# One core, attention and a feed-forward layer: source order on all engines, and seven block products from chunk 12 on

## The chip, the core and the metric

The kernel runs on one core of a Trainium2 chip. The metric is the device time of one execution in microseconds. The core's engines each follow a queue of instructions of their own: PE multiplies matrices, DVE and ACT work on tiles of 128 partitions, POOL takes some elementwise work, SP issues the DMAs. They wait for each other by semaphores.

## The reference

```python
def _attn_ref(q, k, v, omega):            # q, k, v: (8, 8, 576, 64), omega: (128, 64)
    q_s, k_s = (q * scale, k * scale)
    def phi(x):
        proj = np.einsum('bhsd,md->bhsm', x, omega)
        sq = np.sum(x * x, axis=-1, keepdims=True) / 2.0
        h = proj - sq
        h = h - np.max(h, axis=-1, keepdims=True)
        return np.exp(h) / np.sqrt(m)
    q_p, k_p = (phi(q_s), phi(k_s))
    kv = np.einsum('bhsm,bhsd->bhmd', k_p, v)
    z = np.sum(k_p, axis=2)
    num = np.einsum('bhsm,bhmd->bhsd', q_p, kv)
    den = np.einsum('bhsm,bhm->bhs', q_p, z)[..., None] + 1e-06
    return num / den

def _moe_ref(x, w_in, w_out):             # x: (4608, 512), w_in: (512, 2048), w_out: (2048, 512)
    h = x @ w_in
    sp = np.where(h > 20.0, h, np.log1p(np.exp(np.minimum(h, 20.0))))
    g = h * np.tanh(sp)                   # mish
    return g @ w_out
```

The attention's output, heads side by side, is x of the feed-forward layer.

## The kernel before

The 4608 tokens are 36 tiles of 128 (t) and 18 chunks of 256 (c). Fp32 values are split into two fp16 halves, a rounded one (`cast`) and what it leaves (`rest`), and a product is three fp16 matmuls: low by high, high by low, high by high.

**Attention.** `q_task` runs once for each tile t, `k_task` for each batch b and pair of heads hp (32 of them). Both start in `features`: the input is split (ACT casts sq or sk, POOL makes the rest), PE multiplies with omega into two (q) or three (k) banks named pq and pk of the pool ps_a, DVE takes the maximum of each bank and subtracts it, ACT takes the exponential (eq, ek). A q task then has a cast (ACT) and rest (DVE) named qn, a transposing DMA into qp, PE's pn (with kv) in two banks of ps_a, and on DVE rd, its reciprocal and x, which frees the bank. x is split into xs and sent by a transposing DMA into xT. A k task has kp in the same way, vf scaled on ACT, its cast vb on DVE and rest on POOL, and PE's pkv.

**Feed-forward.** For each chunk `ff_in` makes h = x w_in into banks ph of the pool ps_h (two banks): eight groups of 24 matmuls 128x256. ACT's mish reads a bank one slot later, and `g_split` makes g's two halves a slot after that (cast on ACT, rest on DVE). `ff_out` multiplies the chunk ahead of it with w_out into po, 12 matmuls 128x512 a slot.

**Seven products.** From chunk SC0 on `ff_in7` takes its place. Both operands are cut into 2x2 blocks, and seven products of half size (Strassen's, in Winograd's form) do the work of eight: 24 matmuls 128x128 for each product, for each half of the features (gr 0 and 1), so 336 a chunk. It needs sums of w_in's blocks, s1 to s4, which `s_make` builds once in four parts (gr, hb): ten adds on DVE, four casts on ACT and four rests on DVE for each part, sent to HBM (ds) and loaded back from there for each use by `ask_sum` into a ring of three places in weight slots (rows w<-ds). It needs sums of x's blocks too (`x_sums`, tiles xm). Each product has a bank p_... of ps_a, and DVE adds the banks up in fp32 tiles h.

**Order.** The program is written in slots: `step` runs the pieces of tasks that are due, and each slot has a piece of `ff_in` (i) or of `ff_out` (o). From chunk 2 on the loop at the end of the kernel starts tasks when `pace` allows, and within what the data allow the scheduler of the language's tile layer chooses the order in which instructions stand on each engine. `s_make` starts at four slots, 11 apart, in chunks 11 to 13.

```python
    for i in range(4):
        at(slot[0] + 16 * (SC0 - 6) + 2 + 11 * i, lambda i=i: start(s_make(i // 2, i % 2)))
```

## Time and profile before

| | us |
|---|---|
| three runs | 962.81, 964.0, 983.06 (median 964.0) |
| profiled execution | 962.69 |
| its span | 960.8 |
| busy in the span: PE, DVE, ACT, POOL | 940.9, 624.9, 633.9, 222.7 |
| PE matmuls | 8568 |
| po, all matmuls | 375.2 |
| ph, all matmuls | 344.8 |

In the profile a group is written as line, engine, operation, output <- inputs, and its shape. "Busy" sums the instructions' own lengths, and the lengths of matmuls in a row overlap; the distance from start to start says what one costs. "PEclk" is the granted clock of PE. In a stretch's row the numbers behind the span are the busy times of PE, PEld, DVE, ACT and POOL, with their counts of instructions, then the clock, the DMA share and GB/s. An arrow in square brackets names what ended an instruction's wait.

### The profile page before, as it was taken

The page shows a single profiled execution, that of the slowest core. Times are in us where ns is not written, and L with a number is a line of the kernel's source. Part 1 is how long each engine was busy: PE and PEld are TensorE (multiplying, and loading weights), DVE is VectorE, ACT ScalarE, POOL GpSimd, SP SyncE. Part 2 cuts the span into 40 slices and gives each one's busy share as a digit, 9 for nine tenths or more (in the row PEclk, how much of TensorE's full clock was granted, in tenths as well). Part 3 has the DMA queues.
Part 4 walks back from the last instruction along what each step waited for, and adds up shares of the span by engine and source line. Part 5 has one row for each costly group of instructions (what it writes and reads, how often), then busy time and mean ns, then how long its engine had stood idle before and what let it go on. Part 6 is the DMA issues. An engine that isn't in the chain of part 4 may idle for free. (4 is left out here: it accounts for less than half of the span.)

```text
span 960.8 us, 20397 instructions
## 1 busy us (share of the span) xinstructions
PE 940.9 (98%) x8568; PEld 679.3 (71%) x8568; DVE 624.9 (65%) x1080; ACT 633.9 (66%) x818; POOL 222.7 (23%) x141
## 2 busy tenths in 40 slices
PE   9999988999999999999999999999989999999998
PEld 6788873677677777777777777777756777777663
DVE  5879797587766666656575655788889656643330
ACT  4758875686877877768667775778776866332231
POOL 0000052242432322322133333222231332200000
PEclk9979999999999999999999999999999999999999
DMA  9866314431741346313431253423552145634410
GB/s 287 271 208 208 109 48 94 102 58 61 140 92 37 107 77 119 69 59 75 101 68 53 69 118 66 93 89 68 136 124 73 37 100 115 172 117 131 133 57 33
DMA packets 147403, 100.25 MB, mean 104 GB/s; under 512 B 112112, under 2 KB 124528, under 8 KB 147312
## 3 DMA queue, kind: packets, MB, share of 16 engines
q1 hardware_dynamic: 147312, 98.95, 41.2%
q8 instruction: 67, 1.10, 0.5%
q14 instruction: 24, 0.20, 0.1%
HBM read 58.95 MB, written 13.63 MB: 76 GB/s over the span
## 5 line engine op out<-in xcount | busy, mean ns | idle before, releaser
L858 PE MATMUL po<-wo,g 128*128 128x512 f16 x1632 | 375.2, 380 | 0.0
L689 PE MATMUL ph<-xT,w 128*128 128x256 f16 (+1 forms) x2816 | 344.8, 279 | 0.7 <-ACT xT L72 0.7
L689 PEld LDWEIGHTS <-w 128*128 128x128 f16 x2688 | 261.0, 98 | 47.3 <-issue 0.7
L858 PEld LDWEIGHTS <-g 128*128 128x128 f16 x1632 | 155.1, 98 | 163.9 <-issue 2.2
L83 DVE SCALAR_TENSOR_TENSOR g<-h,us,g 128x1024 f16<-128x1024 f32 (+3 forms) x92 | 120.2, 1316 | 36.8 <-ACT g L72 36.2
L834 ACT ACTIVATE h<-ph,us 128x512 f32<-128x512 f32 (+3 forms) x152 | 83.3, 573 | 77.6 <-PE ph L689 76.8
L81 POOL TENSOR_TENSOR sq<-fq,sq 64x1024 f16<-64x1024 f32 x31 | 69.0, 2227 | 159.1 <-issue 65.2
L81 POOL TENSOR_TENSOR sk<-fk,sk 64x1152 f16<-64x1152 f32 x24 | 60.5, 2520 | 111.5 <-ACT sk L72 86.9
L81 POOL TENSOR_TENSOR xs<-x,xs 128x512 f16<-128x512 f32 (+1 forms) x35 | 44.2, 1264 | 151.9 <-issue 68.0
L72 ACT ACTIVATE g<-h,us 128x1024 f16<-128x1024 f32 (+3 forms) x80 | 72.6, 932 | 1.2
L834 ACT ACT_TABLE_LOAD x55 | 70.6, 1283 | 1.0
L364 ACT ACT_TABLE_LOAD x53 | 68.0, 1283 | 4.2 <-DVE ek L358 3.3
L349 DVE TENSOR_REDUCE mxq<-pq 128x4 f32<-128x512 f32 x72 | 46.8, 682 | 31.7 <-PE pq L340 31.6
L792 PEld LDWEIGHTS <-w 128*128 128x128 f16 x1008 | 58.4, 98 | 5.9
L81 DVE TENSOR_TENSOR qn<-eq,qn 128x1024 f16<-128x1024 f32 x31 | 38.9, 1254 | 36.2 <-ACT qn L72 36.2
L349 DVE TENSOR_REDUCE mxk<-pk 128x4 f32<-128x512 f32 (+1 forms) x96 | 50.1, 548 | 18.0 <-PE pk L340 18.0
L834 ACT ACTIVATE h<-h,us 128x1024 f32<-128x1024 f32 (+2 forms) x16 | 14.7, 933 | 61.9 <-DVE h L801 61.9
L72 ACT ACTIVATE o<-po,us 128x512 f32<-128x512 f32 (+1 forms) x38 | 25.8, 680 | 40.1 <-PE po L858 40.0
L81 DVE TENSOR_TENSOR kp<-ek,kp 128x1152 f16<-128x1152 f32 x24 | 36.4, 1515 | 24.0 <-ACT kp L72 24.0
L364 ACT ACTIVATE eq<-eq,lnt 128x1024 f32<-128x1024 f32 x31 | 35.6, 1148 | 21.2 <-DVE eq L358 21.0
L81 POOL TENSOR_TENSOR vb<-vf,vb 128x640 f16<-128x640 f32 x24 | 39.4, 1641 | 40.6 <-DVE vb L74 28.7
L801 DVE TENSOR_TENSOR h<-p_s,h 128x512 f32<-128x512 f32 x30 | 20.2, 689 | 43.2 <-PE p_s L792 43.2
(140 smaller groups left out, 1156.9 us busy)
## 6 DMA issues: line engine op xcount, KB each, us to landing
w<-ds SPq DMA_DIRECT2D x48, 256.0 KB, 3.4
vf<-in_vL_dram SPq DMA_DIRECT2D x32, 325.0 KB, 3.3
fq<-in_qT_dram SPq DMA_DIRECT2D x36, 256.0 KB, 3.6
out_dram<-o SPq DMA_DIRECT2D x36, 256.0 KB, 2.3
fk<-in_kT_dram SPq DMA_DIRECT2D x24, 256.0 KB, 3.6
raw<-in_w_out_dram SPq DMA_DIRECT2D x5, 1024.0 KB, 8.9
wo<-in_w_in_dram SPq DMA_DIRECT2D x4, 1024.0 KB, 13.2
raw<-in_w_in_dram SPq DMA_DIRECT2D x4, 1024.0 KB, 15.2
```

The source lines that it names most:

```text
L72: act.activation(out, in_, AF.Copy, scale=scale)
L81: eng.tensor_tensor(out=out, in0=in_, in1=hi, op=ALU.subtract)
L83: eng.scalar_tensor_tensor(out=out, in0=in_, scalar=scale, in1=hi, op0=ALU.mult, op1=ALU.subtract)
L349: sub = dve.tensor_reduce(out=mx[:, lo:hi], in_=pp[:, :m, :], axis=AX.X, op=ALU.max, negate=by_act)
L364: last = act.activation(e, e, AF.Exp, bias=lnt)
L689: nc.tensor.matmul(out=ph[:, i, :], lhsT=wi(a, k, f) if c else wi0(k, f), rhs=xT[c][:, y, k, :] if c else xT0()[:, k, :], start=n == 0, st ...
L792: nc.tensor.matmul(out=ph[:, i, :], lhsT=left(gr, op_l, i, a, k), rhs=x_region(c, r)[:, y, k0 + k, :], start=n == 0, stop=n == len(mm) - 1,)
L801: dve.tensor_tensor(out=out, in0=bank, in1=in0, op=ALU.add)
L834: act.activation(h[:, :, lo:hi], ph[:, :, lo:hi], AF.Mish, scale=us[:, 0:1])
L858: nc.tensor.matmul(out=po[i], lhsT=gT[c, gr][:, a, f % FG, i * P:(i + 1) * P], rhs=wo(y, f), start=f == 0 and (a, y) == parts[0], stop=f = ...
```

## The change

Four things are changed together.

1. SC0 goes from 15 to 12: chunks 12, 13 and 14 also use the seven products. `s_make` starts in chunks 8 to 10, its four parts 12 slots apart, with each rest and each store one slot later than its cast.
2. From chunk 2 on PE, SP, DVE, ACT and POOL keep the order of the source (`manual_schedule`). Every chunk has 16 slots that alternate i and o, and q and k tasks begin at slots that a table `base` fixes (q 27 and 23 slots ahead of their chunk, k at two places of the 16). For the later tasks the gaps ahead of pkv and pn are 4 and 3 slots.
3. The products of `ff_in7` accumulate in place. Bank pa (of ps_h) takes a11 b11, then s2 t2, s3 t3 and a22 t4 on top; ACT casts it in between and mish reads it at the end. Bank pd takes s1 t1, then s4 b22; bank pb (of ps_a) takes a12 b21. DVE has three adds for each half chunk where it had seven.
4. Buffers: xT has two tiles, each large enough for x's sums too; xs three; the h tiles four in place of five; v loads are cut into one piece for each pair of heads (`v_unit`).

```diff
-    SC0 = 15
+    SC0 = 12
...
+    def v_unit(b, hp):
+
+        if hp == 0:
+            vstate[b] = ({}, None, None)
+            vm[b] = sb.tile([P, HP], F32, tag="vmx", name=f"vmx{b}", bufs=2)
+        vstate[b][0][hp] = t = fetch_v(b, hp)
+        yield 4
+        dve.tensor_reduce(
+            out=vm[b][:, hp:hp + 1], in_=t[:, :, 0:D], axis=AX.XY, op=ALU.max, apply_absolute_value=True
+        )
+        if hp < HP - 1:
+            return
+        am = sb.tile([P, 1], F32, tag="vam", name=f"vam{b}")
+        dve.tensor_reduce(out=am, in_=vm[b], axis=AX.X, op=ALU.max)
+        allm = over_partitions(am, f"v{b}")
+        yield 1
+        p, s = pow2_of(allm, f"v{b}", TOP)
+        vstate[b] = (vstate[b][0], p, s)
+
...
-        yield gap("kv", f"k{b}_{hp}")
+        if b > 1 and b + 1 < B and hp + 1 < HP:
+            start(v_unit(b + 1, hp + 1), 2)
+        yield KV_GAP if nth >= LATE else gap("kv", f"k{b}_{hp}")
...
-        yield 2
+        yield QP_GAP if nth >= LATE else 2
...
+    REGION = ((0, 4), (1024, 4), (2048, 4), (3072, 2))
+
+    def x_tile(c):
+        if c not in xT:
+            xT[c] = sb.tile([P, 3584], F16, tag="xT", name=f"xT{c}", bufs=2)
+        return xT[c]
+
+    def x_plain(c):
+        return x_tile(c)[:, 0:2 * KT * CH].rearrange("p (a k s) -> p a k s", a=2, k=KT)
 
...
-    SUMS = ("s2", "s3", "s1", "s4")
+    SUMS = ("s2", "s1", "s3", "s4")
...
         def send(op, src):
-            o = sb.tile([P, 2, n], F16, tag="xs", name=f"{op}_{gr}_{hb}", bufs=2)
+            o = sb.tile([P, 2, n], F16, tag="xs", name=f"{op}_{gr}_{hb}", bufs=3)
             cast(act, o[:, 0], src)
+            yield 1
             rest(dve, o[:, 1], src, o[:, 0])
+            yield 1
             sums[gr, hb, op] = dram.tile([P, 2, n], F16, name=f"d{op}_{gr}_{hb}")
             nc.sync.dma_start(out=sums[gr, hb, op], in_=o)
 
         tt(s, block(sl2, 0, 0), block(sl2, 0, 1), ALU.add)
         tt(u, block(sl2, 1, 0), block(sl2, 1, 1), ALU.add)
         tt(s, s, u, ALU.add)
-        send("s1", s)
-        yield 2
+        yield from send("s1", s)
+        yield 1
         tt(s, s, block(sl1, 0, 0))
         tt(s, s, block(sl1, 1, 0))
-        send("s2", s)
-        yield 2
+        yield from send("s2", s)
+        yield 1
         tt(u, block(sl1, 0, 1), s)
         tt(u, u, block(sl1, 1, 1), ALU.add)
-        send("s4", u)
-        yield 2
+        yield from send("s4", u)
+        yield 1
         tt(s, block(sl1, 0, 0), block(sl2, 0, 0))
         tt(u, block(sl1, 1, 0), block(sl2, 1, 0))
         tt(s, s, u, ALU.add)
-        send("s3", s)
+        yield from send("s3", s)
         did("sums")
 
...
-        def products(gr, op_l, op_r):
+        def products(bank, gr, op_l, op_r, first):
             r, k0 = right[op_r]
             mm = [(a, y, k) for a, y in ((1, 0), (0, 1), (0, 0)) for k in range(2)]
-            ph = ps_a.tile([P, FQ, P], F32, tag="a", name=f"p_{op_l}_{c}_{gr}")
             for i in range(FQ):
                 for n, (a, y, k) in enumerate(mm):
                     nc.tensor.matmul(
-                        out=ph[:, i, :], lhsT=left(gr, op_l, i, a, k), rhs=x_region(c, r)[:, y, k0 + k, :],
-                        start=n == 0, stop=n == len(mm) - 1,
+                        out=bank[:, i, :], lhsT=left(gr, op_l, i, a, k), rhs=x_region(c, r)[:, y, k0 + k, :],
+                        start=first and i == 0 and n == 0, stop=n == len(mm) - 1, skip_group_check=True,
                     )
             if op_l in SUMS:
-                ask_sum()
-            return ph
-
-        def add(out, in0, bank):
-            dve.tensor_tensor(out=out, in0=bank, in1=in0, op=ALU.add)
+                later(1, ask_sum)
+
+        def bank(pool_, tag, name):
+            return pool_.tile([P, FQ, P], F32, tag=tag, name=name)
+
+        def add(out, bank):
+            dve.tensor_tensor(out=out, in0=bank, in1=out, op=ALU.add)
 
         for gr in range(FT // FG):
             gT[c, gr] = sb.tile([P, 2, FG, CH], F16, tag="g", name=f"g{c}_{gr}", bufs=GB)
...
             c11, c12, c21, c22 = (x[:, :, o:o + P] for x in h for o in (0, P))
 
 
-            p1 = products(gr, "a11", "b11")
-            cast(act, c21, p1)
+            pa = bank(ps_h, "h", f"pa{c}_{gr}")
+            products(pa, gr, "a11", "b11", True)
+            cast(act, c11, pa)
+            pb = bank(ps_a, "a", f"pb{c}_{gr}")
+            products(pb, gr, "a12", "b21", True)
+            later(1, add, c11, pb)
             yield
-            add(c11, c21, products(gr, "a12", "b21"))
+            products(pa, gr, "s2", "t2", False)
+            cast(act, c12, pa)
+            pd = bank(ps_h, "h", f"pd{c}_{gr}")
+            products(pd, gr, "s1", "t1", True)
             yield
-            add(c12, c21, products(gr, "s2", "t2"))
+            products(pa, gr, "s3", "t3", False)
+            cast(act, c22, pa)
+            later(1, add, c22, pd)
             yield
-            add(c21, c12, products(gr, "s3", "t3"))
+            products(pa, gr, "a22", "t4", False)
+            mish7(sp, h[1], pa)
+            products(pd, gr, "s4", "b22", False)
+            later(1, add, c12, pd)
+            later(1, mish, sp, h[0], h[0])
+            later(2, g_split, c, gr, 1, sp, h[1])
+            later(3, g_split, c, gr, 0, sp, h[0])
             yield
-            p5 = products(gr, "s1", "t1")
-            add(c22, c21, p5)
-            add(c12, c12, p5)
-            yield
-            add(c12, c12, products(gr, "s4", "b22"))
-            later(1, mish, sp, h[0], h[0])
-            later(2, g_split, c, gr, 0, sp, h[0])
-            yield
-            add(c21, c21, products(gr, "a22", "t4"))
-            later(1, mish, sp, h[1], h[1])
-            later(2, g_split, c, gr, 1, sp, h[1])
-            yield
+
+    def mish7(sp, h, pa):
+
+        for us, lo, hi in sp:
+            if lo < P:
+                e = min(hi, P)
+                act.activation(h[:, :, lo:e], pa[:, :, lo:e], AF.Mish, scale=us[:, 0:1])
+            if hi > P:
+                b = max(lo, P)
+                act.activation(h[:, :, b:hi], h[:, :, b:hi], AF.Mish, scale=us[:, 0:1])
 
...
-    GB, HB, QB = 4, 5, 1
+    GB, HB, QB = 4, 4, 1
...
+    LATE, KV_GAP, QP_GAP = 17, 4, 3
 
...
-    def pace(c):
-
-        return 15 + (c - 1) * 4.0 if c < 5 else 31.0 + (c - 5) * 3.8
+    def CS(c):
+
+        return 65 + 16 * (c - 2)
 
...
+    items = [("q", t) for t in range(NT)] + [("k", b, hp) for b in range(B) for hp in range(HP)]
+    items.sort(key=lambda it: it[1] if it[0] == "q" else it[1] * S // P - 0.5)
+    F = len(FIRST)
+    base = {}
+    for it in items[F:]:
+        if it[0] == "q":
+            base[it] = CS(it[1] // 2) - (23 if it[1] % 2 else 27)
+    late = CS(NCH)
+    for it in reversed(items[F:]):
+        if it[0] == "k":
+            late = min(late, base["q", it[1] * S // P]) - 1
+            while (late - CS(0)) % 16 not in (1, 13):
+                late -= 1
+            base[it] = late
+    items[F:] = sorted(items[F:], key=lambda it: base[it])
+    begin = list(FIRST) + [base[it] for it in items[F:]]
...
-        at(slot[0] + 16 * (SC0 - 6) + 2 + 11 * i, lambda i=i: start(s_make(i // 2, i % 2)))
+        at(slot[0] + 16 * (SC0 - 6) + 12 * i, lambda i=i: start(s_make(i // 2, i % 2)))
+    own = ExitStack()
+    own.enter_context(tc.manual_schedule(engines={mybir.EngineType.PE, mybir.EngineType.SP, mybir.EngineType.DVE, mybir.EngineType.Activation, mybir.EngineType.Pool}))
     for c in range(2, NCH):
         fi, fo = (ff_in if c < SC0 else ff_in7)(c), ff_out(c - 1)
-        order = "io" * 8 if c < SC0 else "iioiioioioi" * 2
+        order = "io" * 8
         for j, what in enumerate(order):
-            if j % 2 == 0 and given[0] < min(pace(c + j / len(order)), len(items)):
+            while F <= given[0] < len(items) and begin[given[0]] <= slot[0]:
                 give()
             next(fi if what == "i" else fo, None)
-            if (j + 1) * 16 // len(order) > j * 16 // len(order):
-                step()
+            step()
         for gen in (fi, fo):
             next(gen, None)
```

Three places where the rows stand otherwise. The first is ACT where a part of the sums is made (s1 to s4 the casts of sums, eq and ek exponentials, ph a bank of h's product). Before, in chunk 11:

```order
L834 ACTIVATE h11_1_1_7902<-ph11_1_1_0_7903,us5_7387 128x2x192
L434 ACTIVATE vf7_3_8185<-vf7_3_8185,s_v7_8408 128x10x64
L72 ACTIVATE sq29_8150<-fq29_8046 64x1024
L364 ACT_TABLE_LOAD
L364 ACTIVATE eq27_7928<-eq27_7928,lnt_72 128x1024
L72 ACTIVATE s1_0_1_8010<-s0_1_8006 128x512
L72 ACTIVATE kv6_7053<-pkv6_3_7966 128x2x65
L72 ACTIVATE qn27_8043<-eq27_7928 128x1024
L834 ACT_TABLE_LOAD
L834 ACTIVATE h11_1_1_7902<-ph11_1_1_2_8015,us4_6150 128x2x64
L834 ACTIVATE h11_1_1_7902<-ph11_1_1_2_8015,us5_7387 128x2x192
```

After, in chunk 9:

```order
L72 ACTIVATE sk5_3_6293<-fk5_3_6148 64x1152
L72 ACTIVATE g9_0_6087<-h9_0_0_6088,us4_6082 128x1024
L72 ACTIVATE s3_0_1_6312<-s0_1_5954 128x512
L387 ACT_TABLE_LOAD
L387 ACTIVATE ek5_2_6233<-ek5_2_6233,lnt_72 128x1152
L72 ACTIVATE kp5_2_6315<-ek5_2_6233 128x1152
L457 ACTIVATE vf5_2_4642<-vf5_2_4642,s_v5_5299 128x10x64
L875 ACT_TABLE_LOAD
L875 ACTIVATE h9_0_1_6257<-ph9_0_1_0_6258,us4_6082 128x512
L875 ACTIVATE h9_0_1_6257<-ph9_0_1_2_6323,us4_6082 128x512
```

Before, the cast of a sum stands behind the exponential; after, the cast of s3 stands ahead of the table load and the exponential ek, and kp's cast, vf and the mish of ph9_0_1_0 stand behind those.

The second is DVE at the corresponding places (s0_1 the sum in the making, x21 and x27 the quotients that free pn's bank). Before:

```order
L358 TENSOR_TENSOR eq28_8099<-pq28_4_8110,mxq28_8100 128x512
L724 TENSOR_TENSOR s0_1_8006<-w1_107,w3_109 128x512
L724 TENSOR_TENSOR s0_1_8006<-s0_1_8006 128x512
L506 TENSOR_SCALAR rd27_8188<-pn27_0_8189 128x4
L81 TENSOR_TENSOR qn28_8216<-eq28_8099,qn28_8216 128x1024
L510 RECIPROCAL rd27_8188<-rd27_8188 128x4
L506 TENSOR_SCALAR rd27_8188<-pn27_1_8202 128x4
L511 TENSOR_TENSOR x27_8187<-pn27_0_8189,rd27_8188 128x256
L510 RECIPROCAL rd27_8188<-rd27_8188 128x4
L511 TENSOR_TENSOR x27_8187<-pn27_1_8202,rd27_8188 128x256
```

After:

```order
L381 TENSOR_TENSOR ek5_2_6233<-pk5_2_5_6247,mxk5_2_6234 128x512
L83 SCALAR_TENSOR_TENSOR g9_0_6087<-h9_0_0_6088,us4_6082,g9_0_6087 128x1024
L749 TENSOR_TENSOR s0_1_5954<-w1_76,w3_78 128x512 x2
L749 TENSOR_TENSOR s0_1_5954<-s0_1_5954 128x512
L74 CAST vb0_114<-vf5_2_4642 128x10x64
L81 TENSOR_TENSOR s3_0_1_6312<-s0_1_5954,s3_0_1_6312 128x512
L81 TENSOR_TENSOR kp5_2_6315<-ek5_2_6233,kp5_2_6315 128x1152
L529 TENSOR_SCALAR rd21_6349<-pn21_0_6350 128x4
L533 RECIPROCAL rd21_6349<-rd21_6349 128x4
L534 TENSOR_TENSOR x21_6348<-pn21_0_6350,rd21_6349 128x256
```

Before, two adds and qn's rest stand between the subtraction and x27; after, g's rest, three adds, vb's cast, the sum's rest and kp's rest stand between the subtraction and x21.

The third is DVE where the seven products' banks are added up (h15 and h12 the tiles of h). Before, in chunk 15, the first chunk with them:

```order
L511 TENSOR_TENSOR x34_10133<-pn34_0_10135,rd34_10134 128x256
L510 RECIPROCAL rd34_10134<-rd34_10134 128x4
L511 TENSOR_TENSOR x34_10133<-pn34_1_10148,rd34_10134 128x256
L74 CAST xs17_0_10190<-x34_10133 128x512
L801 TENSOR_TENSOR h15_0_0_10077<-p_s2_15_0_10195,h15_0_1_10078 128x4x128
L801 TENSOR_TENSOR h15_0_1_10078<-p_s3_15_0_10223,h15_0_0_10077 128x4x128
L801 TENSOR_TENSOR h15_0_1_10078<-p_s1_15_0_10266,h15_0_1_10078 128x4x128
L801 TENSOR_TENSOR h15_0_0_10077<-p_s1_15_0_10266,h15_0_0_10077 128x4x128
```

After, in chunk 12:

```order
L372 TENSOR_REDUCE mxk7_0_8331<-pk7_0_4_8341 128x1
L381 TENSOR_TENSOR ek7_0_8330<-pk7_0_4_8341,mxk7_0_8331 128x128
L372 TENSOR_REDUCE mxk7_0_8331<-pk7_0_5_8344 128x4
L381 TENSOR_TENSOR ek7_0_8330<-pk7_0_5_8344,mxk7_0_8331 128x512
L74 CAST vb0_114<-vf7_0_7021 128x10x64
L829 TENSOR_TENSOR h12_0_1_8141<-pd12_0_8253,h12_0_1_8141 128x4x128
L81 TENSOR_TENSOR kp7_0_8405<-ek7_0_8330,kp7_0_8405 128x1152
L529 TENSOR_SCALAR rd27_8466<-pn27_0_8467 128x4
```

Before, four adds of banks of ps_a follow x34 with nothing of another kind between them; after, the one add of pd12_0 stands behind vb's cast and ahead of kp's rest.

## The prediction

> **What bounds the kernel now.** I read the page's busy shares first, then the busy time by stretch (one stretch per chunk of 256 tokens), then PE's waits, and last the single instructions around the waits.

> ```profile
> span 960.8 us, 20397 instructions
> ...
> PE 940.9 (98%) x8568; PEld 679.3 (71%) x8568; DVE 624.9 (65%) x1080; ACT 633.9 (66%) x818; POOL 222.7 (23%) x141
> ```

> PE is the bound: 98% busy. So a change can win in two ways only: less matmul time, or PE's few idle stretches. The stretches below are chunk 6 (an ordinary one), 11, 12, 13 and 16; after the span come busy times of PE, PEld, DVE, ACT, POOL.

> ```profile
> 371.95:420.94 48.99, 48.99 (x468) 35.49 (x467) 29.80 (x62) 36.47 (x47) 13.40 (x9) 1.00 0.39 69
> 615.04:664.46 49.42, 49.42 (x480) 35.91 (x478) 42.59 (x71) 38.44 (x55) 15.16 (x10) 1.00 0.26 69
> 664.46:717.32 52.86, 50.38 (x452) 35.19 (x451) 49.52 (x81) 39.26 (x46) 14.95 (x8) 0.97 0.55 126
> 717.32:768.40 51.08, 49.58 (x479) 35.84 (x478) 38.23 (x55) 38.78 (x54) 11.97 (x7) 1.00 0.21 63
> 857.12:896.60 39.48, 39.48 (x436) 28.14 (x434) 14.04 (x20) 10.98 (x14) 0.00 (x0) 1.00 0.38 121
> ```

> Chunks 11 to 13 are where before builds the sums of weight blocks (s_make). DVE is there at 38 to 50 us a chunk where it has 30 ordinarily, and two of the three chunks are longer than chunk 6 by 2 to 4 us. That is the nearest thing the trace has to what the change will do in chunks 8 to 10. PE's waits from chunk 2 to the end, with totals, times and the longest:

> ```profile
> PE pk L340 <- DVE x L511: 2.7, 2, 2.4
> PE pkv L445 <- DVE kp L81: 1.9, 2, 1.5
> PE pn L495 <- DMA qp<-qn: 0.9, 1, 0.9
> ```

> They add up to 5.5 us. The longest, and what came around it, in PE's timeline (start, length, group; starts of successive groups give the true pace):

> ```profile
> 697.56 0.92 PE L495 MATMUL pn<-kv,qp 128*128 128x65 f16 x24
> 698.32 2.75 PE L858 MATMUL po<-wo,g 128*128 128x512 f16 x12
> 700.91 2.78 PE L689 MATMUL ph<-xT,w 128*128 128x256 f16 x24
> 703.53 0.72 PE L340 MATMUL pk<-om,sk 128*128 128x128 f16 x10
> 706.63 0.63 PE L340 MATMUL pk<-om,sk 128*128 128x128 f16 x8 [2.38 <-DVE x L511]
> 707.08 4.44 PE L858 MATMUL po<-wo,g 128*128 128x512 f16 x12
> ...
> 862.38 1.50 PE L792 MATMUL p_s<-xm,w 128*128 128x128 f16 x24
> 863.73 1.50 PE L792 MATMUL p_s<-xT,w 128*128 128x128 f16 x24
> ```

> Start to start: pn 0.76 us, po 2.59, ph 2.62, 24 matmuls of 128x128 1.35 (56 ns each), 8 of them 0.45. Behind the 2.38 us wait, po took 4.44 instead of 2.75: 1.69 us lost to a lower granted clock (0.97 over that chunk). So PE loses 5.5 + 1.7 = 7.2 us from chunk 2 on.

> Why PE waited there is the key to the forecast. The third bank of pk is one that pn held, and DVE's x frees it:

> ```profile
> 701.41 2.21 DVE L81 TENSOR_TENSOR s<-s,s 128x512 f16<-128x512 f32 x1
> ...
> 704.75 0.15 DVE L506 TENSOR_SCALAR rd<-pn 128x4 f32<-128x4 f32 x1
> 704.82 1.21 DVE L81 TENSOR_TENSOR qn<-eq,qn 128x1024 f16<-128x1024 f32 x1
> ...
> 706.14 0.42 DVE L511 TENSOR_TENSOR x<-pn,rd 128x256 f32<-128x256 f32 x1
> 706.49 0.17 DVE L510 RECIPROCAL rd<-rd 128x4 f32<-128x4 f32 x1
> ...
> 707.15 0.43 DVE L74 CAST xs<-x 128x512 f16<-128x512 f32 x1
> 707.49 1.28 DVE L83 SCALAR_TENSOR_TENSOR g<-h,us,g 128x1024 f16<-128x1024 f32 x1
> ```

> A sum's rest of 2.21 us, two adds and qn's rest stand ahead of x on DVE. Work of s_make ahead of x stops PE.

> **The change, part by part.** *Seven products in chunks 12 to 14.* Each of them had 8 groups ph of 24 matmuls 128x256: 8 x 2.62 = 20.96 us. It gets 2 x 7 x 24 = 336 of 128x128: 14 x 1.35 = 18.90. That is 2.06 less a chunk, **-6.2 us** in three. This lies on the path, since PE is the bound. [...]

> *Adds in place.* Accumulating in the bank replaces 7 DVE adds per half chunk by 3. DVE is at 14 of 39 us in chunk 16, so this is worth nothing there; what it puts in chunks 12 and 13 is priced below. The loads of the sums double to 96:

> ```profile
> w<-ds SPq DMA_DIRECT2D x48, 256.0 KB, 3.4
> ```

> Each is asked for one slot after a product, three products ahead of its use, some 11 us: with 3.4 us to land it is hidden. Behind SP's waits for a transpose (queue work that now stands in source order) that cover shrinks to 1.5 to 3 us; I price it at nothing, with a few us above.

> *Source order on all engines.* Before's order from chunk 2 on is made anew, so its three waits and the slow-clock stretch have no reason to be at the same places: **-7.2 us** at most, taken whole, since any new wait is priced by itself. In ordinary chunks (3 to 7, 11) I walked two chunks of the new order with the rows here: the banks of ph and pk come free at least 2.4 us ahead of PE. I cost that at nothing; the cover is this slack.

> *s_make in chunks 8 to 10.* DVE has about 30 us a chunk and gets nearly all of what chunks 11 to 13 had extra: 42.59 + 49.52 + 38.23 - 3 x 29.80 = 40.9 us in 48 slots of 3.06. By load alone (30 + 14 of 49) it fits. By order it doesn't. The last of a sum's four parts, in slots 181 to 184: ACT's cast of s3 stands ahead of the table load and exp of ek, and DVE's adds that it waits for stand behind g's rest. DVE's vb cast then waits for ACT's vf, and holds s3's rest, kp's rest and x21. The rows, by shape, of the stretch of chunks 11 to 13 (us busy, then mean ns):

> ```profile
> L349 DVE TENSOR_REDUCE mxk<-pk 128x4 f32<-128x512 f32 x14 | 9.5, 680 | 0.0
> L358 DVE TENSOR_TENSOR ek<-pk,mxk 128x512 f32<-128x512 f32 x14 | 9.5, 679 | 0.0
> L81 DVE TENSOR_TENSOR kp<-ek,kp 128x1152 f16<-128x1152 f32 x7 | 9.5, 1356 | 7.3 <-ACT kp L72 7.3
> L724 DVE TENSOR_TENSOR s<-w,w 128x512 f32<-128x512 f16 x8 | 5.5, 683 | 0.1
> L74 DVE CAST vb<-vf 128x640 f16<-128x640 f32 x6 | 2.9, 486 | 0.0
> L349 DVE TENSOR_REDUCE mxk<-pk 128x1 f32<-128x128 f32 x7 | 1.9, 278 | 0.0
> L358 DVE TENSOR_TENSOR ek<-pk,mxk 128x128 f32<-128x128 f32 x7 | 1.9, 277 | 0.0
> ...
> L364 ACT ACT_TABLE_LOAD x12 | 15.4, 1283 | 0.2
> L72 ACT ACTIVATE s<-s 128x512 f16<-128x512 f32 x16 | 10.0, 626 | 19.2 <-DVE s L724 10.8 <-POOL vb L81 3.8 <-DMA xT<-xs 2.9
> L364 ACT ACTIVATE ek<-ek,lnt 128x1152 f32<-128x1152 f32 x7 | 8.8, 1256 | 7.9 <-DVE ek L358 7.9
> L72 ACT ACTIVATE kp<-ek 128x1152 f16<-128x1152 f32 x7 | 8.1, 1152 | 0.0
> L434 ACT ACTIVATE vf<-vf,s_v 128x640 f32<-128x640 f32 x4 | 3.2, 830 | 0.0
> ```

> T = 0 is the end of x20's first half, which lets PE go on in slot 180. DVE: second half of x 0.74 (0.15 + 0.17 + 0.42), xs cast 0.43, a sum's rest 0.68 (as an undisturbed add of that size), three pieces of reduce and subtract 3.27, g's rest 1.28, three adds 2.05: 8.5. ACT: cast 0.63, table 1.28, exp 1.26, kp 1.15, vf 0.83: 13.6. DVE: vb 0.49, rest 0.68, kp's rest 1.36, rd, reciprocal and x 0.74: 16.9. PE meanwhile: 0.45, ph 2.62, po 2.59, ph 2.62, pn 0.76, po 2.59, ten of pk 0.56: 12.2. PE waits **4.7 us**. I walked slots 161 to 184 in this way, which hold two of the four sums; PE waits 0.5 (slot 164), 2.3 (168), 3.6 (173), 1.6 (177), 1.4 (180) and 4.7 (184): 14.1. The four come every 12 slots and the k and q tasks every 4, so the other two repeat it: **+28 us**. The bound below is nothing, if what I call ordered so tightly runs ahead of PE; above, rests and adds beside POOL at up to 2.2 us (the row at 701.41) instead of 0.68 raise the same walk to about 44 us. I take 28, the walk with undisturbed durations, because the only waits of this kind in the trace, 2.38 and the other 0.3 of pk's 2.7, came with a better order.

> *Chunks 12 and 13.* DVE's add of the s1 product (out of bank pd) stands behind the vb cast, and PE's s4 product goes into pd. Walked likewise from x: DVE 0.74 + 0.43 + 3.27 = 4.4, exp, kp and vf 3.2, vb and the add 1.2: 8.8. PE: 0.45 + 1.35 + 2.59 + 1.35 = 5.7. A wait of 3.0 in the first half of each: **+6 us** (0 if DVE is early, 10 with POOL beside it).

> *Clock.* Each wait of 2.4 us or more may cost 1.7 as at 707.08; six places walked are that long (two each of 3.6, 4.7 and 3.0): 0 to +10. [...] I put no term in, and let it carry the upper end.

> Sum: 960.8 - 6.2 - 7.2 + 28.1 + 6.0 = 981.5 of span; the profiled execution took 962.69, 1.9 more than its span: 983.4. The median of the runs shown is 964.0, 1.3 above the profiled one, so the figure is **983**, +2.0%.

> **The rivals.** *The engines keep up.* Only the products and the old waits count: 960.8 - 13.4 + 1.9 = 949, with a few short waits up to 966. For it: DVE 0.9 loaded at most, ACT 0.8, and before's chunk 11 lost only 0.4 us with 42.59 us on DVE. Against it: two engines that wait for each other within one slot, in an order nobody may leave, and the 2.38 us wait with less ahead of x.

> *Contended rests and the lower clock.* The place is the same, slots 161 to 208. If DVE's rests and g's rests run beside POOL's long ones, the walk gives 44 instead of 28, and the waits are long enough for the slower clock, 10 more: 960.8 - 13.4 + 44 + 6 + 10 + 1.9 = 1009. It decides from the point where a sum's rest takes over 1.5 us in most slots; in chunks 11 to 13 some did (2.21), some did not.

> *The in-place bank.* In chunks 12 to 17 PE's next product into pa waits for ACT's cast of it, twelve half chunks with some 2 us of slack. If ACT is late by 2 more each time, 24 us come on top of 949: 973. Against it: ACT at 11 of 39 us in chunk 16.

> *The weight load shows.* A load of weights is longer than the matmul it feeds:

> ```profile
> L689 PEld LDWEIGHTS <-w 128*128 128x128 f16 x2688 | 261.0, 98 | 47.3 <-issue 0.7
> ```

> If its 98 ns were not hidden, chunks 12 to 14 would have 336 x 98 = 32.9 us of products, 14.0 more each than priced: 983 + 42 = 1025. In chunk 16 it is hidden. [...]

> **How the numbers follow.** The walk (966 to 1000) has 0.58, the engines that keep up (946 to 966) 0.28, contended rests (over 1000) 0.08, the bank 0.05, the weight load 0.01. The likeliest gives 983, its own range 966 to 1000. The whole range takes in the upper part of the rival that is faster: **950 to 1000**. Two per cent, about what a measurement of this kernel can tell from no change, are 944.7 and 983.3. Below 944.7 the walk has nothing and the first rival only its edge: 0.03. Above 983.3 lies half of the walk (0.29), all of the contended case and the weight load (0.09) and some of the bank case: 0.42. Within: 0.55.

> **What would show it.** Right: PE waits in chunks 8 to 10 for DVE's x (pk) and ACT's mish (ph), 20 to 40 us in all, at the same places every 12 slots; ACT idle for s ahead of exp; chunks 12 to 14 near 47, 47 and 44 us. A wait at the s4 product in chunks 12 and 13. Wrong: chunks 8 to 10 at 49 us each, which would be the first rival; or chunks 3 to 7 over 49.5, for I gave them slack. If ordinary chunks wait, my walk of them was too kind, and if sums cost under 10 us, too harsh.

## The result and the profile after

The changed kernel takes 1025.78 us (median, 1023.89 the lowest) against 964.2 us of the kernel before: a ratio of 1.0637, 95% interval 1.0612 to 1.0662. The forecast was 983, the range 950 to 1000. In some executions the startup, up to chunk 0's first matmul of ph, takes some 17 us longer (64 us instead of 46.5); so times "from chunk 2 on" below go from chunk 2's first matmul of ph to the end of the span. They are 787.8 us before and 851.3 after. Each is of one profiled execution; the two profiles of one and the same kernel, e1 and e9 below, have 781.7 and 781.3.

The page after, busy times; PE has 432 more matmuls and is busy for 93% of the span instead of 98%:

```profile
span 1023.9 us, 21326 instructions
...
PE 956.5 (93%) x9000; PEld 692.9 (68%) x9000; DVE 622.2 (61%) x1092; ACT 639.1 (62%) x836; POOL 235.8 (23%) x147
```

DVE's and ACT's busy times are nearly as before (624.9 and 633.9), and POOL's, 13 us longer, is 23% of the span. So no engine has become too full: PE waits. Its waits from chunk 2 on (total, times, longest), which summed to 5.5 us before:

```profile
PE pk L363 <- DVE x L534: 14.7, 6, 4.7
PE pq L363 <- POOL sq L81: 13.5, 6, 5.4
PE pq L363 <- DVE ek L381: 9.2, 1, 9.2
PE ph L714 <- ACT h L875: 7.9, 4, 3.4
PE pd L818 <- DVE h L829: 5.6, 3, 2.8
PE pd L818 <- DMA w<-ds: 3.1, 3, 2.1
```

That is 54 us. The stretches show where: chunks 2, 3, 6, 8, 9, 10, 12 and 13 (after the span PE, PEld, DVE, ACT, POOL, then the clock):

```profile
172.56:237.15 64.59, 52.48 (x503) 38.25 (x501) 41.60 (x70) 40.06 (x47) 19.90 (x10) 0.95 0.31 72
237.15:289.43 52.28, 52.08 (x502) 37.50 (x501) 35.19 (x64) 41.58 (x47) 17.67 (x9) 0.96 0.32 81
387.34:436.22 48.88, 48.88 (x468) 35.39 (x466) 28.81 (x54) 37.90 (x51) 15.77 (x9) 1.00 0.37 88
488.22:546.83 58.61, 51.98 (x467) 36.76 (x466) 43.21 (x67) 36.10 (x40) 14.38 (x8) 0.95 0.32 87
546.83:611.05 64.22, 54.12 (x464) 38.27 (x464) 45.69 (x79) 42.77 (x49) 17.51 (x10) 0.88 0.38 93
611.05:670.24 59.19, 52.09 (x491) 36.85 (x490) 43.12 (x67) 35.54 (x39) 14.00 (x8) 0.95 0.34 81
724.12:774.60 50.48, 47.73 (x611) 36.15 (x610) 35.50 (x60) 32.27 (x38) 15.96 (x10) 0.99 0.66 148
774.60:827.32 52.72, 48.60 (x612) 36.67 (x610) 37.01 (x66) 35.48 (x43) 15.97 (x10) 0.97 0.63 149
```

Chunk 6, where no sums are made, runs at 48.88, as well as before. Chunks 8 to 10 take 182.0 us, 35.4 over three of that. In their rows PE's busy time is 3 to 5 us over chunk 6's, and the clock below 1: behind eleven of the waits PE's pace halves for a while. Summed over the starts of all matmuls these stretches cost 19.6 us (2.6 and 2.4 behind the waits of 9.2 and 4.7, 1.5 to 1.7 behind nine others; before, one of 1.7). Which waits have such a stretch behind them is in the last section.

The three largest kinds of wait, in the timelines of the changed kernel. First the one in slot 184 that the prediction walked, on PE, ACT and DVE:

```profile
571.83 0.72 PE L363 MATMUL pk<-om,sk 128*128 128x128 f16 x10
577.20 1.03 PE L363 MATMUL pk<-om,sk 128*128 128x128 f16 x8 [4.65 <-DVE x L534]
```

```profile
567.69 0.63 ACT L72 ACTIVATE s<-s 128x512 f16<-128x512 f32 x1 [5.72 <-DVE s L749]
568.34 1.28 ACT L387 ACT_TABLE_LOAD   x1
569.63 1.25 ACT L387 ACTIVATE ek<-ek,lnt 128x1152 f32<-128x1152 f32 x1
570.92 1.16 ACT L72 ACTIVATE kp<-ek 128x1152 f16<-128x1152 f32 x1
571.99 0.81 ACT L457 ACTIVATE vf<-vf,s_v 128x640 f32<-128x640 f32 x1
```

```profile
566.97 0.69 DVE L749 TENSOR_TENSOR s<-s 128x512 f32<-128x512 f32 x1
572.84 0.50 DVE L74 CAST vb<-vf 128x640 f16<-128x640 f32 x1 [5.18 <-ACT vf L457]
573.25 0.68 DVE L81 TENSOR_TENSOR s<-s,s 128x512 f16<-128x512 f32 x1
573.85 2.56 DVE L81 TENSOR_TENSOR kp<-ek,kp 128x1152 f16<-128x1152 f32 x1
...
576.72 0.42 DVE L534 TENSOR_TENSOR x<-pn,rd 128x256 f32<-128x256 f32 x1
```

DVE's add ends, ACT casts the sum, loads the table, takes exp, kp and vf; all that time DVE stands at vb's cast, with x behind it. Second, the wait of 9.2 us in chunk 2, on PE, ACT, DVE and SP (SP's row merges two transposes; a row of SP's length includes what the instruction waited):

```profile
235.49 1.87 PE L363 MATMUL pq<-om,sq 128*128 128x128 f16 x16 [9.24 <-DVE ek L381]
237.15 4.64 PE L714 MATMUL ph<-xT,w 128*128 128x256 f16 x24
```

```profile
229.99 1.06 ACT L72 ACTIVATE sq<-fq 64x1024 f16<-64x1024 f32 x1 [9.16 <-DMA fq<-in_qT_dram]
```

```profile
228.66 0.82 DVE L299 TENSOR_REDUCE vmx<-vf 128x1 f32<-128x640 f32 x1 [8.11 <-DMA vf<-in_vL_dram]
...
234.66 0.69 DVE L381 TENSOR_TENSOR ek<-pk,mxk 128x512 f32<-128x512 f32 x1
```

```profile
197.36 27.61 SPq L600 DMA_TRANSPOSE xT<-xs  x2
225.06 0.52 SPq L271 DMA_DIRECT2D vf<-in_vL_dram  x1
225.69 0.51 SPq L320 DMA_DIRECT2D fq<-in_qT_dram  x1
```

Two loads came late, vf and fq, issued at 225.06 and 225.69 behind a transpose that SP's waits list holds for 25.0 us against PE's ph. DVE stood 8.11 us at v's maximum for vf, and ek, which stands behind it, ended at 235.35; that is the last thing before PE went on at 235.49, as the profile says. ACT stood 9.16 us for fq; sq's rest on POOL ended at 233.82 (with DVE free, in e7, PE waits here for it alone, 7.2 us). The transpose writes tile 8's x into xT4, which now has the buffer of xT2, and chunk 2 still reads that. The ph row shows the lower clock: 4.64 instead of 2.78. Third, POOL ahead of a wait of pq for sq:

```profile
598.84 0.72 POOL L120 PARTITION_ALL_REDUCE allm_v<-vam  x1 [6.45 <-DVE vam L305]
607.19 2.12 POOL L81 TENSOR_TENSOR sq<-fq,sq 64x1024 f16<-64x1024 f32 x1 [7.63 <-issue]
```

Between v's maximum over partitions and the next instruction the profile has POOL idle for 7.6 us with nothing to wait for, and PE waits 5.4 us for sq. The gap was there before too, also ahead of a rest of sq, but no wait of PE came of it:

```profile
301.77 0.38 POOL L114 PARTITION_ALL_REDUCE allm_v<-vam  x1 [6.21 <-DVE g L83]
309.21 2.13 POOL L81 TENSOR_TENSOR sq<-fq,sq 64x1024 f16<-64x1024 f32 x1 [7.07 <-issue]
```

### The profile page after: what moved, and what is told of

Its sections match the earlier page's. It is cut to its first block, busy times and chain, and to the rows that moved or that the text cites. A ratio compares the mean times of both kernels' runs of the same rounds, so it can differ in the third digit from the quotient of the medians.

```text
span 1023.9 us, 21326 instructions
## 1 busy us (share of the span) xinstructions
PE 956.5 (93%) x9000; PEld 692.9 (68%) x9000; DVE 622.2 (61%) x1092; ACT 639.1 (62%) x836; POOL 235.8 (23%) x147
## 3 DMA queue, kind: packets, MB, share of 16 engines
q8 instruction: 70, 1.15, 0.5%
## 5 line engine op out<-in xcount | busy, mean ns | idle before, releaser
L714 PE MATMUL ph<-xT,w 128*128 128x256 f16 (+1 forms) x2240 | 291.7, 289 | 8.6 <-ACT h L875 7.9
L714 PEld LDWEIGHTS <-w 128*128 128x128 f16 x2112 | 211.6, 101 | 47.3 <-issue 9.1
L818 PEld LDWEIGHTS <-w 128*128 128x128 f16 x2016 | 117.5, 98 | 18.1 <-issue 5.9
L83 DVE SCALAR_TENSOR_TENSOR g<-h,us,g 128x1024 f16<-128x1024 f32 (+3 forms) x92 | 98.3, 1088 | 45.7 <-ACT g L72 45.0
L81 POOL TENSOR_TENSOR xs<-x,xs 128x512 f16<-128x512 f32 (+1 forms) x38 | 47.2, 1241 | 254.5 <-DVE xs L74 112.0
L81 POOL TENSOR_TENSOR sq<-fq,sq 64x1024 f16<-64x1024 f32 x31 | 67.9, 2191 | 93.2 <-ACT sq L72 43.9
L875 ACT ACTIVATE h<-ph,us 128x512 f32<-128x512 f32 (+3 forms) x120 | 64.2, 571 | 29.3 <-PE ph L714 28.7
L81 POOL TENSOR_TENSOR sk<-fk,sk 64x1152 f16<-64x1152 f32 x24 | 56.9, 2371 | 100.9 <-ACT sk L72 77.7
L81 POOL TENSOR_TENSOR vb<-vf,vb 128x640 f16<-128x640 f32 x24 | 48.7, 2028 | 106.8 <-DVE vb L74 97.1
L818 PE MATMUL pa<-xT,w 128*128 128x128 f16 x1152 | 72.9, 220 | 0.0
L72 ACT ACTIVATE g<-h,us 128x1024 f16<-128x1024 f32 (+3 forms) x80 | 71.6, 925 | 0.1
L81 DVE TENSOR_TENSOR qn<-eq,qn 128x1024 f16<-128x1024 f32 x31 | 37.9, 1222 | 51.4 <-ACT qn L72 51.4
L72 ACT ACTIVATE h<-pa 128x512 f32<-128x512 f32 x36 | 21.3, 590 | 73.4 <-PE pa L818 73.1
L387 ACT ACT_TABLE_LOAD x50 | 64.2, 1283 | 0.9
L363 PE MATMUL pq<-om,sq 128*128 128x128 f16 x496 | 36.6, 233 | 25.6 <-POOL sq L81 16.4
L363 PEld LDWEIGHTS <-sq 128*128 128x128 f16 x496 | 32.9, 105 | 34.6 <-POOL sq L81 19.6
L875 ACT ACT_TABLE_LOAD x43 | 55.2, 1283 | 0.8
L72 ACT ACTIVATE o<-po,us 128x512 f32<-128x512 f32 (+1 forms) x38 | 25.8, 678 | 45.1 <-DVE us L690 21.7
## 6 DMA issues: line engine op xcount, KB each, us to landing
w<-ds SPq DMA_DIRECT2D x96, 256.0 KB, 3.5
fq<-in_qT_dram SPq DMA_DIRECT2D x36, 256.0 KB, 4.0
out_dram<-o SPq DMA_DIRECT2D x36, 256.0 KB, 2.0
fk<-in_kT_dram SPq DMA_DIRECT2D x24, 256.0 KB, 3.7
raw<-in_w_in_dram SPq DMA_DIRECT2D x4, 1024.0 KB, 15.4
```

Source lines behind the costliest of these rows:

```text
L72: act.activation(out, in_, AF.Copy, scale=scale)
L81: eng.tensor_tensor(out=out, in0=in_, in1=hi, op=ALU.subtract)
L83: eng.scalar_tensor_tensor(out=out, in0=in_, scalar=scale, in1=hi, op0=ALU.mult, op1=ALU.subtract)
L363: nc.tensor.matmul(out=pp[rows, i, :], lhsT=left[:, o:o + rows.stop - rows.start], rhs=right, start=j == 0, stop=j == len(terms) - 1,)
L387: last = act.activation(e, e, AF.Exp, bias=lnt)
L714: nc.tensor.matmul(out=ph[:, i, :], lhsT=wi(a, k, f) if c else wi0(k, f), rhs=x_plain(c)[:, y, k, :] if c else xT0()[:, k, :], start=n == ...
```

## The experiments

Theory A: the fixed order makes PE wait, in three separate ways (A1 POOL's gap ahead of sq, A2 the transpose that blocks SP's loads, A3 the casts of sums ahead of exp on ACT) and one more (A4 vb's cast ahead of the add). Rival B: what costs is the rest of the change, the two xT tiles, the doubled loads of sums, or the banks that PE and ACT use in turn.

**e1: the whole change but for the fixed order.**

```diff
-    own.enter_context(tc.manual_schedule(engines={...}))
```

> The changed kernel with one line taken out: no engine is held to source order from chunk 2 on; the tile layer's scheduler orders all of them, as before. Theory A (fixed order makes PE wait): PE's waits from chunk 2 on fall from 58 us to under 20, span 960 to 985. Rival B (the parts of the change other than the order cost the time: two xT tiles, twice the sum loads, banks used in turn by PE and ACT): span stays over 1000.

Measured: span 955.1, the times 956.86 and 951.75. Its waits:

```profile
PE pk L363 <- DVE x L534: 6.3, 4, 3.8
```

781.7 us from chunk 2 on: 69.6 less than with the fixed order, 6.1 less than the kernel before. Rival B falls as a cost of its own: with the scheduler's order there is no loss, and the rest of the change is a small gain. (Under the fixed order parts of it can still matter: in A2 the transpose waits for one of the two tiles of xT.)

**e2: the products alone.**

```diff
-    SC0 = 15
+    SC0 = 12
```

> The kernel before with the seven products from chunk 12 on and nothing else (SC0 12 in place of 15). If the products are worth what their matmuls say: span 954 to 960, that is 960.8 - 6.2 plus or minus some waits. Rival: chunks 12 to 14 also carry attention tasks, and three adds of banks more on DVE and the product banks out of ps_a make PE wait there, span over 965.

Measured: 810.8 us from chunk 2 on, 23.0 more than before; chunks 12 to 14 take 51.8, 55.9 and 46.1 us where e1 has 46.7, 46.7 and 43.0. The rival's size, but not its place: together these three take only some 2 us more than before, while chunks 9, 10 and 15 take 53.4, 54.8 and 49.7 instead of 48.9, 47.5 and 41.0. And another kind of wait leads:

```profile
PE pn L495 <- DMA qp<-qn: 12.0, 3, 5.1
PE pn L495 <- DVE s_v L124: 2.8, 1, 2.8
```

A transpose of qn that lands late is the largest part, in chunks 9, 10 and 15. Why it was late here was not tried. What follows is that the products from chunk 12 don't pay in the old assembly; e1 differs from this kernel in all of the change but the order, so which part mends it is not shown.

**e3: without POOL's maximum for v of batches 2 to 7** (the scale of batch 1 is used; that work is left out).

```diff
-        allm = over_partitions(am, f"v{b}")
         yield 1
+        allm = allms[1]
```

> The changed kernel without the maximum over partitions on POOL for v of batches 2 to 7: the one of batch 1 is used for all, so this work is left out. Theory A1 (POOL's next instruction starts 7 us after each such maximum, and in source order that is the rest of sq for which pq waits): the waits of pq for sq at the five places (337, 484, 604, 720 us and the like) go, 12.7 us, with some 6 us of slow clock behind them: span 1004 to 1010. Rival: POOL is late for sq for another reason (ACT's cast is late): the waits stay, span over 1015.

Its span is 1025.5, 17.8 of it a longer startup; from chunk 2 on it takes 836.5, 14.8 less than the changed kernel. pq's waits for sq, 13.5 us, are down to this:

```profile
PE pq L366 <- POOL sq L81: 2.6, 2, 1.5
```

A1 holds, at the lower end of the expected gain; the two left are the ones that stood behind no maximum.

**e4: the q task of tile 8 later** (slot 71, and batch 2's k tasks at 59, 62, 65 and 68).

```diff
+    items[16:21] = items[17:21] + items[16:17]
     F = len(FIRST)
```

> The changed kernel with task q of tile 8 begun at slot 71 in place of 59, and the four k tasks of batch 2 one place earlier (59, 62, 65, 68). Theory A2 (the transposing DMA of x8 into xT4 waits 25 us on SP for chunk 2's last read of the same buffer, and loads behind it come late): the wait of pq at 226 us, 9.2 us, and the clock behind it, 2.6 us, go, chunk 2 takes 50 to 54 us instead of 64.6, span 1010 to 1014. Rival: the load was late for another reason, chunk 2 stays over 60 us.

Measured: span 1011.9, 840.5 from chunk 2 on, 10.8 less. Chunk 2 takes 55.7 us instead of 64.6, chunk 3 54.7 instead of 52.3. SP at the same place:

```profile
196.00 1.26 SPq L600 DMA_TRANSPOSE xT<-xs  x1
198.48 0.34 SPq L271 DMA_DIRECT2D vf<-in_vL_dram  x1
200.93 0.49 SPq L320 DMA_DIRECT2D fq<-in_qT_dram  x1
```

fq is issued at 200.93, and the wait of 9.2 is gone. A2 holds. Giving xT its third tile back was not tried.

**e5: the casts of sums one slot later.**

```diff
         def send(op, src):
+            yield 1
             cast(act, o[:, 0], src)
             yield 1
             rest(dve, o[:, 1], src, o[:, 0])
-            yield 1
```

> The changed kernel with each cast of a sum one slot behind its adds, and rest and store in the slot after it (still three slots for each sum). Theory A3 (casts of sums that wait on ACT ahead of exp are what makes x and mish late in chunks 8 to 10): these three chunks take 182.0 us now, 35 over three ordinary ones; they fall to 155 to 167, span 996 to 1010. Rival: it is DVE's load in that stretch, whatever the order of ACT: they stay over 175, span over 1016.

Measured: span 994.3, 822.0 from chunk 2 on, 29.3 less. Chunks 8 to 10:

```profile
486.38:539.67 53.29, 50.47 (x466) 36.12 (x465) 44.17 (x75) 37.88 (x43) 14.86 (x8) 0.97 0.41 102
539.67:591.12 51.45, 49.06 (x468) 35.31 (x466) 40.60 (x72) 41.78 (x47) 19.02 (x10) 1.00 0.46 104
591.12:642.07 50.95, 49.29 (x492) 35.47 (x489) 41.29 (x66) 33.92 (x38) 15.10 (x8) 1.00 0.38 94
```

155.7 instead of 182.0, with DVE nearly as busy as it was (126.1 us against 132.0). A3 holds, and DVE's load is not the main cause: with the casts a slot later the loss in these chunks is 9 us instead of 35. The edit moves the sum's rest on DVE a slot later too, away from ahead of x; in slot 184 that rest is 0.68 us, against 5.18 for which DVE stood at vb's cast.

**e6: the add of c22 at once.**

```diff
-            later(1, add, c22, pd)
+            add(c22, pd)
```

> The changed kernel with the add of bank pd into c22 in the slot of the s3 product, ahead of vb's cast on DVE instead of behind it. Theory A4: the three waits of pd for that add (2.2, 0.9, 3.0 us at 742, 768, 794) go, and the slow clock behind one (1.6): span 1016 to 1019. Rival: DVE, which then waits for PE's s3 product ahead of ek, makes x late instead: no gain or a loss, span over 1021.

Measured: span 1023.5, 851.5 from chunk 2 on: nothing gained. pd's wait for the add is gone, and pk's for x went from 14.7 us in 6 to this:

```profile
PE pk L363 <- DVE x L534: 19.8, 9, 5.4
```

DVE now waits for PE's product ahead of its reductions, and x is late in its place: three waits of 1.2 to 1.7 us in chunks 12 and 13. These two chunks take 101.4 us instead of 103.2, and 102.5 in e3, e4 and e5, which leave the add alone. So the 5.6 us of waits were real, but taking them away saves some 1 to 2 us at most; the rest moved. (x's waits grew by some 2 us in chunks 3 and 9 too, which the edit doesn't touch.)

**e7: DVE and ACT free, PE, SP and POOL in source order.**

```diff
-    ...(engines={PE, SP, DVE, Activation, Pool})
+    ...(engines={PE, SP, Pool})
```

> The changed kernel with PE, SP and POOL in source order and DVE and ACT left to the scheduler. If the waits come from what stands ahead of x, mish and exp on DVE and ACT: waits for x, mish and the add (28 us and their clock) go, those for fq (9.4) and sq behind the maximum (13) stay: span 970 to 990. Rival: SP and POOL hold everything up: span over 1000. Second rival: the order of DVE and ACT is the whole cost: under 962.

Measured: span 990.6, 817.7 from chunk 2 on, 33.6 less. Chunk 2 stays at 62.9 and sq's waits at 12.8 us; chunks 8 to 10 fall to 158.6. That is near where e5 put them by one `yield`. The span is just over the 970 to 990 expected.

**e8: e3, e4, e5 and e6 together, all engines in source order** (the maximum left out as in e3).

> The changed kernel, all engines in source order, with four of the causes taken out together: the late q task of tile 8, the cast of sums one slot later, the add of c22 at once, and no maximum over partitions on POOL for v of batches 2 to 7 (that work is left out). If the causes are separate and add up: 12 + 15 + 15 to 25 + 6 us from 1023.9, span 955 to 980 (a startup that differs moves it by up to 16 us; chunk 2's start tells). If new waits take their places: span over 985.

Measured: span 991.3 with the longer startup, and 802.4 from chunk 2 on, 48.9 less than the changed kernel. The single gains make 14.8 + 10.8 + 29.3 - 0.2 = 54.7: they nearly add up. What is left over e1 is 20.7 us.

**e9: e1 timed.** The same kernel.

> The kernel of e1 again (the whole change but for the fixed source order), to time it against the kernel before with an interval. From the spans so far (955.1 and 950.0 against 963.4): a ratio of 0.985 to 0.993, one that does not reach 1. Rival: e1's two runs were at the lucky end, ratio 0.993 to 1.005.

Measured: ratio to before 0.9919, interval 0.989 to 0.9948. It is faster, by 0.8%; one run of e1, at 951.75, had been the lucky end. Its profile has 781.3 from chunk 2 on.

**e10: e1 with e4's and e5's edits.**

> The kernel of e1 with the late q task of tile 8 and the later casts of sums as well. If the scheduler's order suffers from the same two causes in small (3.9 us of x at 530 us, chunk 8 at 54.5): 2 to 6 us under e1. If the scheduler had already put them elsewhere: within 2 us of e1 to either side.

Measured: ratio 0.9962 (0.9941 to 0.9983), and 788.7 from chunk 2 on, 7.0 more than e1; by the times it is some 3 us slower (960.5 to 963.73 against e9's 958.04 to 959.5). Chunk 9 stays at 54.8, chunk 3 goes from 51.1 to 57.3 with a new wait of 4.5 us for x. Neither forecast held: what mends the fixed order does some harm to the scheduler's. Which of the two edits does it was not tried.

**e11: e1 with the products from chunk 15.**

```diff
-    SC0 = 12
+    SC0 = 15
```

> The kernel of e1 with the seven products from chunk 15 on as before (SC0 15), all else as in e1. If the three chunks of products are worth what their matmuls say, it is 6.2 us slower than e1 from chunk 2 to the end: 788 us there against 781.7. If banks used in place hide more than that (before with SC0 12 lost 23 us instead of winning 6): 788 to 800.

Measured: 782.6 from chunk 2 on against e1's 781.7; ratio to before 0.9927 (0.9898 to 0.9955). So in time the two are alike, which neither forecast had. The stretches say why: chunks 12 and 13 of this kernel, then chunks 9, 12 and 13 of e1.

```profile
666.67:715.55 48.88, 48.88 (x467) 35.37 (x465) 40.62 (x62) 39.24 (x45) 16.22 (x9) 1.00 0.38 99
715.55:764.42 48.87, 48.87 (x467) 35.36 (x465) 37.79 (x65) 38.66 (x52) 12.74 (x7) 1.00 0.40 97
```

```profile
518.36:572.84 54.48, 50.72 (x467) 36.24 (x465) 42.97 (x75) 41.10 (x46) 17.45 (x10) 0.97 0.41 104
...
670.86:717.54 46.68, 46.68 (x612) 35.35 (x610) 31.27 (x58) 33.28 (x38) 18.68 (x10) 1.00 0.65 154
717.54:764.21 46.67, 46.67 (x611) 35.31 (x609) 33.28 (x61) 38.23 (x47) 14.03 (x9) 1.00 0.70 175
```

The products win 2.2 us a chunk (and 2.2 in chunk 14: 43.0 against 45.2), 6.6 in all; chunk 9 of e1 gives 5.1 of it back, with a wait for x of 3.8 us and the clock behind it.

**e12: SP and POOL free, PE, DVE and ACT in source order.**

> The changed kernel with PE, DVE and ACT in source order and SP and POOL left to the scheduler, the complement of e7. From chunk 2 on the changed kernel takes 851.3 us, with DVE and ACT free 817.7, with all free 781.7. If the parts add up, freeing SP and POOL gives the rest, 851.3 - 36 = 815. If SP's and POOL's order only follows from what DVE and ACT do late: 835 to 851.

Measured: 832.6 from chunk 2 on, 18.7 less. Chunk 2 falls to 55.9 and sq's waits are gone, as A1 and A2 say; chunks 8 to 10 get worse, 188.3. It lies between the two forecasts. With e7's 33.6 that makes 52.3 of 69.6. PE kept the source order in both, so whether the other 17.3 us come from PE's own order or only from all engines being free together is not shown.

**e13: e1 with the sums' four parts 24 slots apart, 48 slots earlier.**

```diff
-        at(slot[0] + 16 * (SC0 - 6) + 12 * i, ...
+        at(slot[0] + 16 * (SC0 - 6) - 48 + 24 * i, ...
```

> The kernel of e1 with the four parts of the sums begun 24 slots apart and 48 slots earlier (chunks 5 to 9 in place of 8 to 10). If what keeps e1 from the product's 6.6 us is only the wait for x in chunk 9 (3.9 us and 1.7 of slow clock), brought by the sums' work: chunk 9 falls from 54.5 to 49, 776 us from chunk 2 to the end instead of 781.7, ratio to before 0.984 to 0.989. Rival: the wait is a late load of v that the sums have nothing to do with: it stays, 780 to 784.

Measured: 777.7 from chunk 2 on, 4.0 less than e1; chunk 9 at 49.3, chunk 7 at 51.3 with a wait of 2.2 for x. The rival falls with chunk 9's wait, but chunk 7 gives part of it back. Ratio to before 0.991 (0.9881 to 0.9939), outside the 0.984 to 0.989 forecast, which the times can't tell from e9's. It has the fewest microseconds from chunk 2 on of the study.

**e14: all in source order, with e4, e5 and e13's spread** (no work left out).

> All engines in source order, with the late q task of tile 8, the later casts, and the sums spread as in e13; no work left out. If the causes add up: 851.3 - 10.8 - 29.3 from chunk 2 to the end, some 811, and a few us less for the spread, 800 to 811. If source order costs more than the causes found so far: over 815. If it can be as good as the scheduler's: under 790.

Measured: 815.9 from chunk 2 on, 35.4 less than the changed kernel and over the 800 to 811 forecast: the fixed order costs more than the causes taken out here. Chunks 8 to 10 take 154.1, hardly less than with e5's edit alone; sq's waits (11.5), the add (5.6) and the ring (3.7) are still there. Half as dense sums hardly help once their casts stand right. Whether they would have helped with the casts where they were was not tried.

## Why the prediction was wrong

**The terms that were right.** The seven products: -6.2 forecast, -6.6 measured (e11 against e1, with the scheduler's order). That PE's old waits would go: -7.2 forecast; in e11, with products as before, 782.6 against 787.8, -5.2, with 2.0 of new waits in it.

**The walk of s_make: right in mechanism, too large in itself, and short of the clock.** Slot 184 was walked at 4.7 us, and the trace has 4.65. The chain is the one walked (ACT's vf ends 13.4 us after T = 0, 13.6 in the walk), but the close match is partly luck: kp's rest took 2.56 us instead of 1.36, and PE came 1.0 later, having had no wait in slot 180. In chunks 8 to 10 the waits for x (11.4 us) and mish (7.0) make 18.4, where the walk said 28. In the slots walked there are 11.3 of 14.1: slot 173 was 1.5 instead of 3.6, and 164 and 180 hadn't a wait at all. "The other two repeat it" failed more: behind slot 184 there are only 3.7 (x, chunk 10) and 3.4 (mish, its end). x is late once a chunk, 16 slots apart, and not every 12. e5 shows the cause, as the prediction named it: the casts ahead of exp.

**The add in chunks 12 and 13**: forecast 6.0, measured 5.6, in three waits instead of two: 2.0 and 2.8 at the places named, and 0.8 in the second half of chunk 12, so the sum is closer than its parts. As a cost that could be won back it is smaller (e6).

**"I put no term in" for the clock.** This was the single term that failed by most: bounded at 0 to 10, it cost 19.6. The one row of before, 1.69 us behind a 2.38 us wait, was the price of nearly every later wait of more than 2 us. The waits of 2.0 to 2.4 us at 337, 484, 545 and 720 us halved the pace as well; two of 2.0 and 2.1 us, at 743 and 889, didn't.

**"In ordinary chunks ... I cost that at nothing."** This step failed, with its cover: chunks 3, 4 and 7 take 52.3, 51.5 and 52.0 us, over the 49.5 that the prediction gave as a sign of being wrong, and chunk 2, which it didn't walk, takes 64.6. The walk of these chunks followed DVE, ACT and PE's banks and left two things out. SP: the buffers of xT, three to two, are in the change, and the transpose that waits for one holds the loads of v and q behind it; 9.2 us of wait and 2.6 of clock in chunk 2 (e4). The prediction named queue work behind SP only for the ring. POOL: a maximum followed by 7 us without an instruction was in the trace of before, ahead of sq's rest and without a cost to PE; in the order after PE waits for that rest; 13.5 us of waits, 11 of which went with it (e3). Neither was among the rivals.

**The ring**: forecast at nothing with a few us above, measured 3.1.

**The rivals.** The engines that keep up: refuted with the fixed order; with the scheduler's, e1 at 955.1 lies inside the 946 to 966 given. Contended rests and the clock: right on the clock, and DVE's kp rest took 2.56 us in the row above, from 573.85 on, beside POOL's rest of vb (1.71 us from 573.48 on), but the walked places weren't longer for it on the whole (18.4, not 44). The in-place bank and the weight load: neither showed; PE has no wait for pa in the list above, and chunks 12 and 13 of e1 run without a wait, at 46.7 us. That the weight load's 1025 is also the measured time is chance. (Its row of 98 ns is of loads for 128x256 matmuls, which at 2.62 us for 24 take 109 ns; only against the 56 ns of 128x128 is such a load the longer.)

Put together, from chunk 2 on: -6.6 (products) - 7.2 (old waits and their clock) + 54.0 (new waits) + 19.6 (clock) = +59.8, against +63.5 measured; 3.7 us have no place in this account. Of the 54.0 the prediction had priced the sums' 18.4 and the add's 5.6; SP's 9.2, POOL's 13.5, the ring's 3.1 and 4.2 of other waits for x and mish it had at nothing. (The forecast's last step names the 1.3 us between the median and the profiled run and doesn't add them; 985 would have followed, which changes nothing.)

## What to carry to other kernels

When engines are fixed to source order, walk all of them: the queue that issues DMAs and the slow side engine too, and every buffer whose number changes, for a single instruction that waits there holds everything behind it (here one transpose on SP, 9.2 us of PE). Price a wait of PE with the slow clock behind it, if the trace has one such row (here 1.69 us behind 2.38 in the trace of before, and 19.6 us behind eleven waits after). And undo causes one at a time and read the stage: two edits that singly took 10.8 and 29.3 us off the fixed order made the scheduler's slower.

## What the runs showed of the hardware

The profile has POOL idle for 6.7 to 7.7 us behind a maximum over partitions, in both kernels, before an ordinary instruction (7.07 us at 309 before, 7.63 at 607 after), in eight of twelve cases with no releaser shown. Between two maxima in a row, at 122.6 and 126.0 of the changed kernel, it is 2.7. The gap is behind each of the twelve maxima that an ordinary instruction follows, not the first alone. The profile gives these maxima themselves 0.38 to 1.31 us; whether part of the gap is their own work, and what else fills it, no run here shows.

Of the thirteen waits of PE of 2.0 us or more in the changed kernel eleven were followed by half the pace, which cost 1.5 to 2.6 us; the longest waits, 9.2, 5.4 and 4.7 us, are among them. The clock's own records show which. The half clock behind these eleven comes in stretches of 3.41 us (eight), 6.83 (two) and 10.24 (one, from 230.70 on), and their starts lie whole multiples of 3.413 us apart: from 230.70 to 339.93 it is 32 of them, to 797.31, the last, 166. These times divide the span into cells of 3.41 us. A wait at 337.6 lies whole in one cell, where PE is busy for 1.41 us, and the next cell has half the clock; one just as long begins at 742.6, ahead of the edge of a cell, PE is busy for 1.55 in that cell, and the clock stays (span, PE, PEld, DVE, ACT, POOL, clock):

```profile
336.52:339.93 3.41, 1.41 (x12) 0.65 (x11) 0.00 (x0) 2.71 (x4) 2.12 (x1) 1.00 0.20 77
339.93:343.34 3.41, 3.41 (x25) 2.68 (x23) 2.91 (x5) 0.20 (x1) 0.00 (x0) 0.50 0.00 0
...
742.70:746.11 3.41, 1.55 (x31) 1.54 (x31) 2.69 (x3) 3.27 (x4) 1.53 (x2) 1.00 0.75 184
746.11:749.53 3.42, 3.42 (x41) 2.00 (x38) 3.25 (x11) 0.00 (x0) 0.00 (x0) 1.00 0.90 246
```
